# A gated convolution on one core: fifteen six-step groups instead of thirteen, one written list for all engines, and a wait between GpSimd's sums

## The chip, the cores and the metric

The kernel runs on one core of one Trainium2 chip. The metric is the device time of one execution in microseconds. Three runs of the kernel before gave 263.25, 263.71 and 264.98 us, a median of 263.71.

## The reference: what is computed

A WaveNet layer: a causal convolution over time with three taps at a dilation of 2, a gate, and a product with an output matrix. `x` is 2 x 16000 x 256, `w` is 3 x 256 x 512, `w_o` is 256 x 256, all bf16.

```
xp = jnp.pad(x, ((0, 0), (4, 0), (0, 0)))
h = xp[:, 4:4 + T] @ w[0]
for i in range(1, 3):
    off = 4 - i * 2
    h = h + xp[:, off:off + T] @ w[i]
f, g = h[..., :256], h[..., 256:]
return (jnp.tanh(f) * sigmoid(g)) @ w_o
```

## The kernel before

The time steps are cut into groups, and the convolution is not computed tap by tap but from sums and differences of input rows, which saves products. A group of kind B takes 4 rows of time at each of up to 256 places (R), 1024 time steps, and needs four products: `first` from the operand `m`, `last` from `p`, `zero` from `d0`, `inf` from `d3`. A group of kind A takes 6 rows at 256 places, 1536 steps, and needs five: `first` from `u1`, `mid` from `rm`, `last` from `rp`, `zero` from `r0`, `inf` from `ri`. The first group, of kind P, is computed tap by tap (`direct`). Before there are 13 A, 12 B (10 of them full, one of 160 and one of 128 places) and P.

Each group has four blocks, one for each 128 of the 512 output columns of `w`. A block is the unit of the schedule. On TensorE it has the products F (first), M (mid, A only), L (last), Z (zero) and I (inf), two matmuls each (`product`, line 401). The first four add up in one PSUM bank `b`, and between them the other engines take readings of it. After F, ScalarE copies `b` to `ss` (token c, line 432). After M, VectorE makes `hh` = 1.5 ss - b (h). After L, VectorE makes `a` = 3 ss + b in another bank (token a of the VectorE column), and `yy` = 2 hh + b (y). I adds into `a`. The rows of the output are then the bank `b` after Z, `yy` and `a`, through tanh or sigmoid on ScalarE (b, y, a; line 475). VectorE multiplies the two halves to `zz` (the gate, g, line 494). P is the output product, `zz` with `w_o`, four matmuls into `o_ps` (line 512). ScalarE casts it to `osb` (e, line 537), or VectorE does (v, line 521), and the SP queue stores it.

The operands come from a transposed input tile `xt`, which the SP queue loads. `m`, `p`, `d0`, `d3`, `u0`, `u1`, `u2`, `e`, `f` are sums or differences of two views of `xt`. `u3`, `uh`, `ud` are multiples of `u1`. `rp` is f + u1, `rm` is e + u3, `r0` is u0 + uh and `ri` is u2 + ud, each written on top of its first term (so in the profile rp's tile is named f, rm's e, and r0's and ri's u). Sums run on VectorE whole, or on GpSimd in quarters of 128 x 256 (`pre`, line 382). `rm`, `rp` and `r0` are made by an accumulating DMA that GpSimd issues (line 377), 13 of each; `ri` is made by GpSimd's sums.

The order is written by hand in PLAN. Each of its lines is the slot of one block and has four columns, for TensorE, ScalarE, VectorE and GpSimd. A block goes through several slots: F in its own, L in the next, Z and I in the one behind. `hold` makes a GpSimd sum wait for a given VectorE instruction: the last one before it in the program, or with one or two marks ' an earlier one. The blocks of the 25 groups of kinds A and B are taken in turn: four B groups first, then A and B mixed about two to one, the last B group at the end.

Of the kernel before, what the change touches and what calls it, by code (L numbers as in the profile page):

```python
# [11 lines left out]

PLAN = """
 |  | m.0 d3.0 p.0 d0.0 G | 
F D D | c w |  | 
F L D | c d | a d3.1 G | wa.4 wa.3
F L Z I P P | c b e | a | wa.6
Z L F I | a b c | m.1 d0.1 p.1 a | wa.12'
F L Z I | a c b | m.2 g a | wa.5
L P F Z I | a e c b | d3.2 a | wa.2'  # L20
Z L F I | a b c | d0.2 u0.0 g a | wa.7
F L Z I | a c b | f.0 u1.0 a | wa.1
L F Z I | a c b | p.2 a u2.0 g | wa.14'
L Z F I P | a b e c | e.0 d3.3 a | wa.0
F P P Z L I | a c e e b | p.3 ud.0 g a | wa.11
L F I Z P P | a c b | u1.1 m.3 m.4 a | rp.0 ri.0'
F L Z P I P | a e e e b c | u3.0 e.1 uh.0 a d0.3 f.2 g | wa.10
F I Z L P | a c e b | u1.2 a | rm.0 ri.0'
L F Z I | a e c b | a g | r0.0
L Z I F P | a b c | u3.1 p.4 a | wa.8  # L30
Z L F P I | a b c e e | u0.1 uh.2 f.1 a d0.4 g | ri.0'
F I L P Z M P | c e a b | d3.4 u2.1 ud.1 a h | rp.1 rm.1 wa.15' wa.13' wa.9'
F Z L M I | a c e e b | g uh.1 a y h | d3.5' d3.5' ri.0'
P P Z F L I | y a b c | u3.2 e.2 a y | r0.1 ri.1 m.5
F L I Z M | a c y b | a u0.2 h | d0.5 d0.5
Z F L I M | a b c e | g a y h | r0.2 d0.5 ri.1
F P Z I L | a e c b y | g u2.2 a y | rm.2 ri.1 m.5' d0.5
F L P I Z M | a e c y b | a e.3 h | p.5
Z F I L M | a c b | g a y h | p.5 p.5 ri.1
P P F Z L I | a e e y c b | u0.3 a y | m.5 m.5'  # L40
L F I Z M | a c y b | ud.2 a u1.3 h | ri.2 ri.2'
Z P P F L I P M | a b e c e e | g u3.3 a y h | rp.2 p.5' p.6' d0.6'
F Z I L P | a e b c y | f.3 g a y | ri.2 d3.5
F L I Z M | a c y b | a u2.3 h | d3.5
Z F I L M P P | a c b e | g a y h | rp.3 rm.3 d0.6 ri.2
F Z I L P | a e e y b c | uh.3 e.4 ud.3 a y | d3.6 p.6 ri.3''
F L I Z M | a c y b | a u1.4 h | ri.3
Z F I L M P P P | a c b e | g a y h | m.6 d3.6
F Z P L I | a e y c b e e e | g u0.4 u3.4 f.4 a y | r0.3 ri.3 m.6''
F L P I Z M | a c y b | a ud.4 h | d0.6 d3.6 m.6  # L50
Z I F L | a b c | g a y | ri.3 m.6
F L P I Z M P | c a y b | u2.4 a h | ri.4' d3.6
F Z L I P M | a e e c b | e.5 uh.4 y a h | rp.4 p.6
F Z P L I | a y c b e e | g f.5 a y | rm.4 p.6' d0.6'
F P L Z M I | a c y b | g a h | r0.4 p.7 p.7 ri.4 d3.7 d3.7 m.7
F Z L P M I | a c e b e | u1.5 a y h | ri.4
I Z P L F P P | a e e b c y | u0.5 a y | ri.4
F L Z I M | a c b y | ud.5 u1.6 u2.5 a h u3.5 g | rp.5 ri.5''
F P Z L I P M | a c e e b | a y h | rm.5 d0.7 p.7
F Z I L P | a e y b c e | g uh.5 a y | m.7' ri.5  # L60
F L I Z P M | a c y b | g ud.6 a h | r0.5 ri.5' m.7'
F P Z L M I | a c b e e | e.6 uh.6 y a h | d3.7 d0.7
F P Z L I P | y e a b c | f.6 a y | m.7' ri.5
F L Z M I P | a c y b e | u0.6 g h u3.6 a | rp.6 p.7' d0.7' d0.7
F L P M Z I | a c e e e b | y a h | rm.6
Z I L F P | a y b c | u2.6 u1.7 a y g | m.8' m.8'
F P P L Z M I | a c e y b e e | g u3.7 a h | r0.6 ri.6' d3.7'
F Z L P I M | a c b | e.7 ud.7 a y h | p.8' ri.6' ri.6
F Z I L P P | a y b c | u0.7 u2.7 a y | p.8' ri.6'
F L P M Z I | a e c y e e b | uh.7 f.7 a h g | d0.8' ri.7'  # L70
Z I F L | a b c | u1.8 a y | rm.7 rp.7 m.8'
F P P L Z M I | a c e y b e | g a e.8 h | d3.8 ri.7
F Z I L M P | a c b e | g a y ud.8 h | p.8 d3.8 ri.7
F P Z I L P | a e c y b e | u3.8 f.8 a y | r0.7 d3.8' d0.8
L F I Z M P | a e c b y | a u0.8 h | d0.8 m.8
F Z P L P M I P | a c e e e b | e.9 g a y h | p.8 ri.7
Z F L I | a b c y | u1.9 g a y | rp.8 d3.8
F L I Z M P P | a c e b y | u2.8 ud.9 a h | rm.8 d0.8 d3.9'
Z F L P M P I P | a e c e e b | uh.8 g a y h | ri.8 ri.8
Z L F I | y a b e c | u3.9 u2.9 a y | r0.8 ri.8  # L80
F I Z L M P P | a c y b | f.9 u0.9 a h | ri.9' ri.8'
F L Z I M | a e e c b | g y a h | ri.9
F Z I L | y a b c e | f.10 g a y | rp.9 d0.9
F P P L Z M I | c a b y | u0.10 a h | rm.9 d0.9'
F Z I L P P M | a e c e b | e.10 g uh.9 y a h | r0.9 d3.9
F P Z L P I | a e e y b c e | m.9 u1.10 a y | ri.9' ri.9
F L I Z M P | c a e b y | p.9 a h | d0.9' d3.9' d3.9'
Z P F L I M | a b c e e | ud.10 g a y h | d0.9
F I Z P L P | a y b c | u2.10 g a y | rp.10 ri.10 d3.10 d0.10
F L I Z M | a c e y b | a u1.11 h |   # L90
Z P F L P I | a b c e | u3.10 g y uh.10 a | rm.10 ri.10'
F L P Z I M | a e c b e y | e.11 a u2.11 h | ri.10'
F I Z L P P M | c a e b | ud.11 f.11 a y u3.11 h | r0.10 ri.10'
F I Z L | a e c y b e | g uh.11 a y | d3.10 d0.10'
L P F P Z M I | a c b y | g a h | rm.11 d0.10 d3.10
F Z L I M P | a c e b | u1.12 a y h | ri.11' ri.11'
F Z I L | a e c b y | p.10 m.10 y a | rp.11 ri.11
L P F P Z M I | a c e b y e | a u3.12 u0.11 h f.12 g | d3.10
Z F P L I P M P | a c b e | a y h | r0.11 ri.11 d0.10
I F Z L P | a e y e b e c | g e.12 ud.12 y a | rm.12  # L100
F P P M Z L P I | c e a b y e | p.11 u2.12 uh.12 a h g | d3.11' ri.12'
F I L P Z M P | a c e b | y a h | d0.11 d3.11
F Z L P I | y e a b c e e | u0.12 m.11 a y | rp.12 r0.12 ri.12''
F P Z L M I | c a b y | a h g | 
F Z L P I M P | a c b e e e | a y h | d0.11 ri.12
F Z L P I | a c b e y | g a y | d3.11 ri.12
L F I Z M P | a c y b e e | a g h | 
Z F L P I P M | b c a | y a h | 
F P Z L I | a e e y b c e | y a | d0.11
F P L Z M I | c a b y | a h g | d0.11  # L110
F P L Z I P | a e c b e | a y | d3.11
F I Z L | a c y b | g a | 
L P I F Z P | a e b c e | a g | 
Z I F L P P | a c b E | a v | 
L Z I P p | a b | a g v | 
Z I P p P | a e b | v | 
H H | a e E | g v | 
R R |  |  | 
 | e | v | 
# [4 lines left out]
def kernel(  # L124
# [7 lines left out]

    nc = tc.nc
# [15 lines left out]
    LOAD = 15  # L151
# [4 lines left out]
    LEAD, TRAIL = 4, 0  # L156
    N_A = (6, 7)
    groups, of_kind = [], {"P": [], "A": [], "B": []}

    def group(kind, b, t, R):  # L160
        of_kind[kind].append(len(groups))
        groups.append(dict(kind=kind, b=b, t0=t, R=R, J=ROWS[kind]))
        return t + ROWS[kind] * R

    for b in range(B):
        t = 0
        if b == 0:
            t = group("P", b, 0, 160)
        rows = (T - t - 6 * RG * N_A[b]) // 4
        n_a, n_b = N_A[b], rows // RG - (0 < rows % RG < P)  # L170
        for n in range(max(n_a, n_b)):
            if n < n_b:
                t = group("B", b, t, RG)
            if n < n_a:
                t = group("A", b, t, RG)
        rows = (T - t) // 4
        while rows:
            t = group("B", b, t, 160 if rows % P else P)
            rows = (T - t) // 4
    As, Bs = of_kind["A"], of_kind["B"]  # L180
    mixed = [[(g, oi) for g in gs for oi in range(4)] for gs in (As, Bs[LEAD:-1 - TRAIL])]
    seq = [(g, oi) for g in Bs[:LEAD] for oi in range(4)]
    took = [0, 0]
    while took != [len(m) for m in mixed]:
        nxt = 0 if took[0] * len(mixed[1]) < took[1] * len(mixed[0]) else 1
        seq.append(mixed[nxt][took[nxt]])
        took[nxt] += 1
    seq += [(g, oi) for g in Bs[-1 - TRAIL:] for oi in range(4)]
    slot_of = {blk: n for n, blk in enumerate(seq)}
    N = len(seq)  # L190
    assert N == 4 * (len(groups) - 1) == len(slot_of)
    begin = {g: slot_of[g, 0] for g in As + Bs}
    end = {g: slot_of[g, 3] for g in As + Bs}
# [323 lines left out]
    def out_evict(g, rb0, jp, on_v=False):  # L517
# [205 lines left out]
```

## Time and profile before

| what | value |
|---|---|
| median of three runs | 263.71 us |
| span of the profiled execution | 261.4 us |
| what lies around the span, median less span | 2.3 us |
| TensorE busy | 256.5 us, 98% |
| ScalarE busy | 243.7 us, 93% |
| VectorE busy | 240.5 us, 92% |
| GpSimd busy | 136.2 us, 52% |

The profile was taken of one execution; its own time outside the span is not shown, so the difference of the median and the span stands for it. An engine's busy time counts the time in which at least one of its instructions is shown at work. Instructions of one engine overlap by some 0.1 us, so the sum of the durations is larger than the busy time, and the distance between the starts of two neighbours is what one takes of its engine.

### The profile page before, as it was taken

The page shows a single profiled execution, that of the slowest core. Times are in us where ns is not written, and L with a number is a line of the kernel's source. Part 1 is how long each engine was busy: PE and PEld are TensorE (multiplying, and loading weights), DVE is VectorE, ACT ScalarE, POOL GpSimd, SP SyncE. Part 2 cuts the span into 40 slices and gives each one's busy share as a digit, 9 for nine tenths or more (in the row PEclk, how much of TensorE's full clock was granted, in tenths as well). Part 3 has the DMA queues.
Part 4 walks back from the last instruction along what each step waited for, and adds up shares of the span by engine and source line. Part 5 has one row for each costly group of instructions (what it writes and reads, how often), then busy time and mean ns, then how long its engine had stood idle before and what let it go on. Part 6 is the DMA issues. An engine that isn't in the chain of part 4 may idle for free.

```text
span 261.4 us, 4534 instructions
## 1 busy us (share of the span) xinstructions
PE 256.5 (98%) x1484; PEld 144.2 (55%) x1484; DVE 240.5 (92%) x401; ACT 243.7 (93%) x492; POOL 136.2 (52%) x204
## 2 busy tenths in 40 slices
PE   8999999999999999999999999999999999999993
PEld 5654565545545555555555555555555555665682
DVE  2899999999999999999999999999999999977773
ACT  4989998999999999999999999999999999999993
POOL 1033355687765577956757685643746453431100
PEclk9999999999999999999999999999999999999999
DMA  6999979999969667969895799959825574462115
GB/s 185 215 168 212 262 177 174 227 211 179 212 152 232 139 147 143 228 147 230 197 197 135 175 214 190 239 160 201 237 41 127 149 152 116 129 160 109 76 61 210
DMA packets 81663, 45.20 MB, mean 173 GB/s; under 512 B 68936, under 2 KB 70216, under 8 KB 81640
## 3 DMA queue, kind: packets, MB, share of 16 engines
q1 hardware_dynamic: 75112, 33.74, 54.6%
q0 software_dynamic: 5616, 10.23, 23.2%
q10 hardware_dynamic: 912, 0.95, 1.1%
q8 instruction: 11, 0.18, 0.3%
q14 instruction: 12, 0.10, 0.1%
HBM read 1.25 MB, written 16.38 MB: 67 GB/s over the span
## 4 chain that ended last, share of the span: by engine, by line
PE 97%; DMA 1%; DVE 0%; issue 0%
PE b L401 57%; PE o_ps L512 21%; PE a L401 16%; PE b L421 1%; PE a L421 1%; DMA xn<-in_x_dram 1%; PE tp L308 0%; DVE osb L521 0%; PE fill L248 0%
## 5 line engine op out<-in xcount | busy, mean ns | idle before, releaser
L435 DVE SCALAR_TENSOR_TENSOR a<-ss,b 128x512 f32<-128x512 f32 (+2 forms) x100 | 67.1, 672 | 7.9 <-ACT sg L475 3.1
L537 ACT CAST osb<-o_ps 128x512 bf16<-128x512 f32 x119 | 69.8, 622 | 0.8 <-PE o_ps L512 0.7
L512 PE MATMUL o_ps<-wo_sb,zz 128*128 128x256 bf16 x496 | 70.5, 273 | 0.0
L432 ACT COPY ss<-b 128x512 f32<-128x512 f32 (+2 forms) x100 | 59.6, 597 | 4.6 <-PE b L401 3.5
L512 PEld LDWEIGHTS <-zz 128*128 128x128 bf16 x496 | 48.4, 98 | 25.2 <-DVE zz L494 0.2
L401 PEld LDWEIGHTS <-w_sb 128*128 128x128 bf16 x400 | 39.0, 98 | 36.8 <-issue 0.2
L382 POOL TENSOR_TENSOR u<-u,ud 128x256 bf16<-128x256 bf16 x52 | 39.8, 772 | 24.9 <-DVE zz L494 9.1
L382 POOL TENSOR_TENSOR d<-xt 128x256 bf16<-128x256 bf16 (+2 forms) x56 | 33.4, 606 | 32.7 <-DVE zz L494 13.0
L494 DVE TENSOR_TENSOR zz<-th,sg 128x1536 bf16<-128x1536 bf16 (+2 forms) x52 | 40.9, 788 | 0.5 <-ACT sg L475 0.2
L435 DVE SCALAR_TENSOR_TENSOR yy<-hh,b 128x512 f32<-128x512 f32 x52 | 35.4, 680 | 1.9 <-PE b L401 1.8
L435 DVE SCALAR_TENSOR_TENSOR hh<-ss,b 128x512 f32<-128x512 f32 x52 | 35.4, 681 | 1.2 <-PE o_ps L512 0.5
L475 ACT ACTIVATE sg<-b 128x512 bf16<-128x512 f32 (+2 forms) x50 | 30.5, 610 | 2.1 <-PE b L401 1.4
L475 ACT ACTIVATE th<-b 128x512 bf16<-128x512 f32 (+2 forms) x50 | 30.5, 610 | 1.9 <-PE b L401 1.6
L475 ACT ACTIVATE sg<-a 128x512 bf16<-128x512 f32 (+2 forms) x50 | 31.0, 619 | 0.0
L401 PE MATMUL b<-f,wp_sb 128*128 128x512 bf16 x104 | 30.9, 379 | 0.0
L401 PE MATMUL b<-u,w_sb 128*128 128x512 bf16 x104 | 30.9, 379 | 0.0
L401 PE MATMUL a<-u,w_sb 128*128 128x512 bf16 x104 | 30.9, 379 | 0.0
L401 PE MATMUL b<-u,wa_sb 128*128 128x512 bf16 x104 | 30.9, 379 | 0.0
L401 PE MATMUL b<-e,wm_sb 128*128 128x512 bf16 x104 | 30.9, 378 | 0.0
L475 ACT ACTIVATE th<-a 128x512 bf16<-128x512 f32 (+2 forms) x50 | 30.5, 614 | 0.3 <-PE a L401 0.2
L401 PEld LDWEIGHTS <-wp_sb 128*128 128x128 bf16 x200 | 19.5, 98 | 20.1 <-issue 0.7
L401 PEld LDWEIGHTS <-wm_sb 128*128 128x128 bf16 x200 | 19.5, 98 | 17.0 <-issue 0.4
(59 smaller groups left out, 342.7 us busy)
## 6 DMA issues: line engine op xcount, KB each, us to landing
out_dram<-osb SPq DMA_DIRECT2D x26, 384.0 KB, 2.6
out_dram<-osb SPq DMA_DIRECT2D x23, 256.0 KB, 3.0
f<-u POOLq DMA_DIRECT2D x13, 256.0 KB, 3.5
e<-u POOLq DMA_DIRECT2D x13, 256.0 KB, 4.4
u<-uh POOLq DMA_DIRECT2D x13, 256.0 KB, 5.3
w_sb<-in_w_dram ACTq DMA_DIRECT2D x3, 256.0 KB, 4.1
xt<-in_x_dram SPq DMA_TRANSPOSE x25, 7.2
xn<-in_x_dram SPq DMA_DIRECT2D x1, 160.0 KB, 3.2
```

What stands on the lines that cost most here:

```text
L382: ins = eng.tensor_tensor(out=o, in0=a, in1=b, op=op)
L401: nc.tensor.matmul(G[bank, oi][:, :2 * R], lhsT=wmat[:, ct, osl], rhs=G[mv][:, :, ct, :R], start=which == "first" and ct == 0, stop=ct == ...
L421: nc.tensor.matmul(G[bank, oi][:, :4 * r].rearrange("p (j r) -> p j r", j=4), lhsT=w_taps[tap][:, ct, osl], rhs=xt[:, j0:j0 + 4, ct, c0 + ...
L432: nc.scalar.copy(out=G["ss", oi][:, :n], in_=G["b", oi][:, :n])
L435: return note(nc.vector.scalar_tensor_tensor(out=out, in0=in0, scalar=scalar, in1=in1, op0=ALU.mult, op1=op))
L475: nc.scalar.activation(out=G[name, dt][:, j:j + 2, :R], in_=G[bank, oi][:, :2 * R].rearrange("p (q r) -> p q r", q=2), func=(ACT.Tanh, ACT ...
L494: note(nc.vector.tensor_tensor(out=G["z"][:, dt, :, :n], in0=G["th", dt][:, :, :n], in1=G["sg", dt][:, :, :n], op=ALU.mult))
L512: nc.tensor.matmul(o_ps[:, q, :], lhsT=z, rhs=wo_sb[:, dt, :], start=dt == 0 and (q == 0 or len(dts) == NT), stop=dt == NT - 1, skip_group ...
L537: copy(out=osb[:, 2 * jp:2 * jp + 2, :], in_=o_ps[:])
```

## The change

**Groups.** The table GROUPS sets them: in the first batch P, seven A, four full B and one B of 128 places; in the second eight A, three full B and one B of 160. That makes 15 A, 9 B (7 of them full) and P, 96 blocks instead of 100. ORDER gives the turn of the blocks: three B groups first, then A and B mixed three to one, the B of 128 at the end.

**One list.** PLAN is now one list of tokens for all engines, 1744 of them, in the order in which the program issues them. A token with a point names an operand: `u1.5q1` is one quarter of u1 of the sixth A group on GpSimd, which waits for the VectorE instruction that stands one back from the last; `rp.13d` is an accumulating DMA; `u3.4` is made by VectorE. In the list are also the loads (x) and the stores (s). Two lines of it:

```diff
+h51 e.14q53 P b I A u2.13q19 e96 L y f.13q26 F s37 Y Z a u0.14q15 I b A P rp.13d c F a rp.14d L c Z ri.13d A I r0.13
+b Z y M u3.14 v97 F b e.14q1 a P h52 I u2.14q14 y F c g e.14q54 L e98 P Y c M e99 d3.8q30 A P e.14q96 y M h53 s38 P
```

**Who does what.** `hh` is made by VectorE as before in 34 of the 60 blocks of kind A. In the other 26 (k) ScalarE copies `b` to `hh`, and VectorE makes `yy` = a - 2 hh, which reads the bank `a` before I adds to it. VectorE casts 28 outputs instead of 5. More of the sums of `xt` run on GpSimd, and `ri` is an accumulating DMA in 14 groups: there are 55 such DMAs instead of 39.

**The wait on GpSimd.** `settle` makes the second sum behind a DMA's issue wait for the end of the first.

**Buffers.** The pools of the operands are replaced by rings with the same number of places (`slot`), and the first weights' parts `wu` take the places of the first `zz` tiles instead of those of `hh` and `yy`.

```diff
+GROUPS = (
+    "P160 A A A A A A A B B B B B128",
+    "A A A A A A A A B B B B160",
+)
...
+    on_pool = []
+
+    def settle(ins, piece):
+
+        if piece and len(on_pool) > 1 and on_pool[-1][1] and not on_pool[-2][1]:
+            tc.add_manual_dep(
+                ins.ins, on_pool[-1][0].ins.name,
+                mybir.DependencyInfo(mybir.DependencyClass.Sync, mybir.DependencyReason.DATA),
+                reason="GpSimd's cores come together behind a DMA's issue",
+            )
+        on_pool.append((ins, piece))
+        return ins
...
-        if name in BY_DMA:
-            return nc.gpsimd.dma_start(out=G[name][:, :, :, :R], in_=b, accum_op=op)
+                G[name] = slot(name, G["n"], [P, 2, CT, RG])
+        if eng is None:
+            return settle(nc.gpsimd.dma_start(out=G[name][:, :, :, :R], in_=b, accum_op=op), False)
...
+        if eng is nc.gpsimd:
+            settle(ins, True)
         return hold(ins, behind)
...
-    def halfway(blk):
+    def second(blk, on_act):
...
-        G["hh", oi] = ss_pool.tile([P, 2 * RG], f32, name="hh")
+        G["hh", oi] = slot("hh", a_seq.index(blk), [P, 2 * RG], f32)
+        if on_act:
+            G["k", oi] = True
+            nc.scalar.copy(out=G["hh", oi][:, :n], in_=G["b", oi][:, :n])
+            return
...
-            stt(G["y", oi][:, :n], G["hh", oi][:, :n], 2.0, b)
+            if ("k", oi) in G:
+                stt(G["y", oi][:, :n], G["hh", oi][:, :n], -2.0, G["a", oi][:, :n])
+            else:
+                stt(G["y", oi][:, :n], G["hh", oi][:, :n], 2.0, b)
...
+    def on_gpsimd(token):
+        token, _, back = token.partition("q")
+        behind = made_v[-1 - int(back)]
...
+        had = quarters.get((g, name), 0)
+        quarters[g, name] = had + 1
+        pre(g, name, nc.gpsimd, slice(had, had + 1), behind=behind)
```

The order on VectorE in the middle of the mixed blocks, before (numbers behind the names tell tiles apart):

```order
L435 SCALAR_TENSOR_TENSOR hh_1433<-ss_1403,b_1400 128x512
L382 TENSOR_TENSOR e_1459<-xt_1049 128x1024
L380 TENSOR_SCALAR uh_1461<-u1_1254 128x1024
L435 SCALAR_TENSOR_TENSOR yy_1463<-hh_1433,b_1400 128x512
L435 SCALAR_TENSOR_TENSOR a_1467<-ss_1403,b_1400 128x512
L435 SCALAR_TENSOR_TENSOR hh_1469<-ss_1442,b_1439 128x512
L494 TENSOR_TENSOR zz_1331<-th_1380,sg_1446 128x1024
L382 TENSOR_TENSOR f_1496<-xt_1049 128x1024
L435 SCALAR_TENSOR_TENSOR a_1501<-ss_1442,b_1439 128x512
```

and a like place now:

```order
L328 TENSOR_SCALAR ud_1235<-u1_942 128x1024
L328 TENSOR_SCALAR uh_1237<-u1_1113 128x1024
L330 TENSOR_TENSOR u2_1243<-xt_820 128x1024
L452 TENSOR_TENSOR zz_1093<-th6_1142,sg6_1178 128x1536
L385 SCALAR_TENSOR_TENSOR a_1265<-ss_1208,b_1193 128x512
L385 SCALAR_TENSOR_TENSOR yy_1276<-hh_1227,a_1265 128x512
L479 CAST osb4_1281<-o_ps_1260 128x512
L385 SCALAR_TENSOR_TENSOR a_1291<-ss_1247,b_1232 128x512
L328 TENSOR_SCALAR ud_1304<-u1_1113 128x1024
L385 SCALAR_TENSOR_TENSOR yy_1309<-hh_1267,a_1291 128x512
```

The sums from SBUF stand together now, and behind them those that read PSUM. The blocks shown have no hh on VectorE, `yy` reads `a` and comes behind it, and a cast stands between.

The order on GpSimd, before, with the semaphores for which each waits:

```order
L382 TENSOR_TENSOR u2_914<-u2_914,ud_1039 128x256 [waits DVE_49]
L382 TENSOR_TENSOR d3_786<-xt_634 128x256
L382 TENSOR_TENSOR d3_786<-xt_634 128x256 [waits DVE_49]
L377 DMA f_1124<-u1_1045 128x1024 [waits DMASW1_49]
L377 DMA e_952<-u3_1089 128x1024 [waits DMASW2_49]
L382 TENSOR_TENSOR d0_1095<-xt_982 128x256 [waits DVE_49]
```

and now:

```order
L325 DMA e_807<-u3_899 128x1024 [waits DMASW4_49,Pool_49]
L325 DMA f_736<-u1_710 128x1024 [waits DMASW5_49,Pool_49]
L325 DMA f_1076<-u1_942 128x1024 [waits DVE_49]
L325 DMA u2_1063<-ud_912 128x1024 [waits DMASW7_49]
L330 TENSOR_TENSOR u1_1113<-xt_820 128x256 [waits DMASW1_49,DMAHW5_49,DVE_49,PE_49]
L330 TENSOR_TENSOR u1_1113<-xt_820 128x256 [waits Pool_49]
L330 TENSOR_TENSOR d3_854<-xt_662 128x256
L330 TENSOR_TENSOR d0_962<-xt_662 128x256
```

Four DMAs are issued in a row, the second sum behind them waits for GpSimd's own semaphore, and the quarters of different operands alternate. Sums that wait for VectorE (DVE) have become fewer: 36 of 172 rows, where it was 89 of 149.

More of the change, by code (lines that the diff above doesn't have):

```diff
@@ L120 @@
+v118 a P e119 Z P e120 P b s46 e121 P g s45 v122 H e123 H R R s47 v124 e125 s48
 """
@@ L209, with slot @@
     ctx.enter_context(tc.manual_schedule())
+    SLOTS = {"m": 2, "p": 2, "d0": 3, "d3": 3, "u0": 3, "u1": 3, "u2": 3, "e": 3, "f": 3, "u3": 2, "uh": 2, "ud": 2, "hh": 3, "th": 2, "osb": 3, "odd": 3}
+    def slot(name, n, shape, dtype=bf16, kind=None):
+        return ring_pool.tile(shape, dtype, name=name, tag=f"{name}.{n % SLOTS[kind or name]}")
     def warm_up(n):
@@ L276 @@
     wm_sb = consts.tile([P, CT, D2], bf16)
-    wu_sb = [[ss_pool.tile([P, D2], f32, name=f"wu{tap}", tag=tag) for tag in ("hh", "yy")] for tap in range(K)]
+    wu_ct = [z_pool.tile([P, K, D2], f32, name="wu", tag="zz6") for _ in range(CT)]
+    wu_sb = [[wu_ct[ct][:, tap, :] for ct in range(CT)] for tap in range(K)]
     wa_sb = consts.tile([P, CT, D2], bf16)
@@ L351, in operand @@
         }[name]()
+    blocks = [0] + [g for g, oi in seq if oi == 3]
+    a_seq = [blk for blk in seq if blk[0] in As]
+    on_pool = []
[8 more added lines that the diff above has]
+        return ins
     def hold(ins, behind):
@@ L362 @@
     ON_TOP = {"rp": "f", "rm": "e", "r0": "u0", "ri": "u2"}
-    BY_DMA = ("rm", "rp", "r0")
     def pre(g, name, eng, qs=slice(0, 4), behind=None):
@@ L465, in activate @@
         if (name, dt) not in G:
-            G[name, dt] = act_pool.tile([P, J, RG], bf16, name=name, tag=f"{name}{J}")
+            same = [at for at in blocks if groups[at]["J"] == J]
+            G[name, dt] = slot(f"{name}{J}", NT * same.index(g) + dt, [P, J, RG], kind="th")
         if G["kind"] == "P":
@@ L705 @@
+    assert next(todo, None) is None and next(to_load, None) is None
 _INS = ['x', 'w', 'w_o']
```

403 lines of the change are left out of this document (141 added, 262 removed).

## The prediction

> **What bounds the kernel now.** I read the page first, for the shares of the engines and the chain that ended last.
>
> ```profile
> span 261.4 us, 4534 instructions
> PE 256.5 (98%) x1484; PEld 144.2 (55%) x1484; DVE 240.5 (92%) x401; ACT 243.7 (93%) x492; POOL 136.2 (52%) x204
> PE 97%; DMA 1%; DVE 0%; issue 0%
> ```
>
> TensorE is busy 98% of the span, and the chain of waits is TensorE for 97% of it. A share over the whole span hides stages, so the busy time in stretches of 20 us comes next. Its columns are the stretch, its length, the busy time and instructions of PE, PEld, DVE, ACT and POOL, the granted clock, the DMA share and GB/s.
>
> ```profile
> 20.00:40.00 20.00, 20.00 (x111) 10.64 (x109) 19.83 (x34) 18.69 (x38) 8.60 (x12) 1.00 1.01 221
> 100.00:120.00 20.00, 20.00 (x114) 10.95 (x113) 19.61 (x32) 19.49 (x40) 15.34 (x22) 1.00 0.84 188
> 180.00:200.00 20.00, 20.00 (x116) 11.14 (x115) 19.52 (x33) 19.30 (x40) 10.57 (x15) 1.00 0.63 152
> 220.00:240.00 20.00, 20.00 (x125) 12.01 (x123) 17.51 (x31) 19.88 (x44) 7.18 (x12) 1.00 0.46 125
> 250.00:261.40 11.40, 7.30 (x67) 6.20 (x64) 6.17 (x12) 7.22 (x19) 0.00 (x0) 0.98 0.41 155
> ```
>
> TensorE never stops between 20 and 240 us, at the full clock. VectorE and ScalarE are nearly as full: 19.5 to 19.8 and 18.7 to 19.9 of 20 us. So three engines are close to the limit, TensorE first, and only GpSimd has room. A little less work on TensorE pays only as long as the other two keep up.
>
> The busy columns count overlapping instructions, so what one instruction really takes of its engine is read from the distance of starts in the timeline:
>
> ```profile
> 99.99 0.69 DVE L435 SCALAR_TENSOR_TENSOR hh<-ss,b 128x512 f32<-128x512 f32 x1
> 100.59 0.68 DVE L494 TENSOR_TENSOR zz<-th,sg 128x1024 bf16<-128x1024 bf16 x1
> 101.19 0.69 DVE L382 TENSOR_TENSOR f<-xt 128x1024 bf16<-128x1024 bf16 x1
> 101.37 1.08 ACT L537 CAST osb<-o_ps 128x512 bf16<-128x512 f32 x2
> 101.45 0.59 PE L401 MATMUL a<-u,w_sb 128*128 128x512 bf16 x2
> 101.88 0.59 PE L401 MATMUL b<-u,wa_sb 128*128 128x512 bf16 x2
> 102.31 0.60 PE L512 MATMUL o_ps<-wo_sb,zz 128*128 128x256 bf16 x4
> 102.31 0.64 ACT L475 ACTIVATE sg<-a 128x512 bf16<-128x512 f32 x1
> 102.80 0.63 ACT L432 COPY ss<-b 128x512 f32<-128x512 f32 x1
> 103.00 0.95 DVE L494 TENSOR_TENSOR zz<-th,sg 128x1536 bf16<-128x1536 bf16 x1
> 103.27 0.69 ACT L475 ACTIVATE th<-yy 128x512 bf16<-128x512 f32 x1
> 103.81 0.64 ACT L475 ACTIVATE th<-b 128x512 bf16<-128x512 f32 x1
> 103.87 0.69 DVE L435 SCALAR_TENSOR_TENSOR a<-ss,b 128x512 f32<-128x512 f32 x1
> ```
>
> Two matmuls of 512 columns take 101.88 - 101.45 = 0.43 us, 0.215 each. A VectorE instruction takes 0.60 (0.87 for the wide gate zz), a ScalarE cast or copy 0.47, an activation 0.49 (0.54 from yy).
>
> **TensorE: the term that carries the sum.** Its products by kind of group, in the groups of lines kept apart by shape:
>
> ```profile
> L401 PE MATMUL a<-u,w_sb 128*128 128x512 bf16 x104 | 30.9, 379 | 0.0
> L401 PE MATMUL a<-d,w_sb 128*128 128x512 bf16 x80 | 23.8, 379 | 0.0
> ```
>
> A six-step group (A) has five products of 8 matmuls, 40 for 1536 rows; 104/8 makes 13 of them. A four-step group (B) has four products, 32 matmuls for 1024 rows; 80/8 makes 10 full ones, with one of 160 and one of 128 columns, which stay. Now there are 15 A and 7 full B: 2x40 more, 3x32 fewer, so 16 matmuls of 512 columns go. The output products stay at 500. 16 x 0.215 = **3.4 us** less, in a stage where TensorE never stops.
>
> **VectorE and ScalarE: both a little less.** By the order, VectorE loses 4 sums into a, 18 of hh, 14 full operand sums (87 to 73) and 6 gates of 1024, and gains 8 sums into yy and 23 casts of outputs: -42 + 31 = -11 at 0.60 is -6.6 us. Six scalings more (their row is below) at 0.34, which is their mean of 0.42 less the 0.08 by which the others overlap, are +2.0, four wide gates at 0.87 are +3.5, small ones about -0.8. Sum: **-1.9 us**. ScalarE loses 23 casts and 4 copies (27 x 0.47 = 12.7) and 8 activations (3.9), and gains 26 copies into hh (12.2) and 8 activations from yy (4.3): **about -0.3 us**, with one small cast.
>
> ```profile
> L380 DVE TENSOR_SCALAR u<-u 128x1024 bf16<-128x1024 bf16 x13 | 5.5, 423 | 0.0
> ```
>
> Neither is on the chain; what they need is shown to be tight by the windows, and that is a rival below.
>
> In 26 of 60 blocks ScalarE's copy replaces VectorE's hh, and yy then reads a. So the "inf" product into a must wait for two VectorE sums (1.2 us) instead of one. In the list it stands at least 0.43 us behind yy's place and mostly 1.3. Bounds: 0 if other products fill this, 26 x 0.17 (0.60 less 0.43) = 4.4 us if all stood at the shortest. Six do, which is 1.0 us; half of it lies within the list's step of 0.43. I take 0.3.
>
> **GpSimd and its DMAs.** Sums on quarters go from 124 wide and 16 small to 140 and 24, accumulating DMAs from 39 to 55 (ri now goes by DMA too). Rows of such a place:
>
> ```profile
> 113.88 0.87 POOL L377 DMA_DIRECT2D e<-u  x1 [1.06 <-DVE u L380]
> 114.54 0.86 POOL L382 TENSOR_TENSOR d<-xt 128x256 bf16<-128x256 bf16 x1
> 115.11 0.91 POOL L382 TENSOR_TENSOR p<-xt 128x256 bf16<-128x256 bf16 x1
> L382 POOL TENSOR_TENSOR u<-u,ud 128x256 bf16<-128x256 bf16 x52 | 39.8, 772 | 24.9 <-DVE zz L494 9.1 <-DVE yy L435 4.4 <-DVE u L382 3.5
> ```
>
> A DMA's issue takes 0.66 us of GpSimd. 24 sums at up to 0.77 and 16 issues at 0.66 add at most 29 us to 136.2: 165 of 261, still with room. The new wait (27 sums name GpSimd's own semaphore) has no row; the sums behind an issue took 0.86 and 0.91 us and started 0.57 apart. At worst the second one starts at the first one's end, 0.3 us later, 27 x 0.3 = 8 us; at best the two no longer stretch each other and it gains 0.2 each. Both lie in GpSimd's room. Behind the waiting sum stand the other quarters and the next DMA's issue, for which a product waits.
>
> That product is the real exposure. From a DMA's place in the list to the first product that reads its tile I counted the product tokens between, at 0.43 us. The shortest are rp.13 with 3.8 us and r0.14 with 3.9, then rm.0, rm.11 and rm.12 with 4.3, rp.2 with 4.8, rm.3 and rm.6 with 5.2; the other 47 have 5.6 and more. The time from issue to landing, from the page:
>
> ```profile
> f<-u POOLq DMA_DIRECT2D x13, 256.0 KB, 3.5
> e<-u POOLq DMA_DIRECT2D x13, 256.0 KB, 4.4
> u<-uh POOLq DMA_DIRECT2D x13, 256.0 KB, 5.3
> DMA to landing us min/median/max: 3.3/4.4/10.9
> ```
>
> At the minimum of 3.3 nothing is late. At the medians rp (f, 3.5) is in time, three rm (e) are 0.1 late each and r0.14 is 1.4 late. r0.14 is the last accumulate, when no input load is left, so it is nearest to the minimum. Bounds 0 and 6.6 us (all eight at 5.3: 1.5 + 1.4 + 3 x 1.0 + 0.5 + 2 x 0.1); I take **0.2**.
>
> The Trainium skill, "DMA: Bandwidth & Descriptors", section "Anatomy of one DMA — SWDGE (gpsimd) path", gives a fit of 2.0 us and the bytes over 436 GB/s. By it 256 KB would land in 2.6 us (an estimate), no DMA would be late, and this term would be 0; the trace's shortest 3.3 is above that, so the trace decides.
>
> **The sum.** The profiled execution's span is 261.4; the runs shown have a median of 263.71, so 2.3 us lie around the span. 261.4 - 3.4 + 0.3 + 0.2 = 258.5, and with 2.3 around it **260.8 us**. The start (direct products of the first group) and the end (last gate, casts, store) are the same steps in both.
>
> **Rivals.** *ScalarE sets the pace.* It had 19.3 to 19.9 of 20 us busy from 100 us on, and keeps its work (-0.3 us) in 1.3% less time. Counting both lists in stretches of eight blocks at the distances above, ScalarE has 0.95 of TensorE's work (0.99 at worst, blocks 32 to 40) against 0.93 before (1.02 at worst). For: the thin margin. Against: the worst stretch is better than before's, which TensorE passed without stopping. If the pace is ScalarE's, only its 0.3 is saved: 263.4 us.
>
> *Accumulating DMAs land late.* This is the slower side. It decides where landing takes over 4.3 us for the five shortest leads; at 5.3 the cost is the 6.6 us above on top of 260.3: 266.9 us, less if the first stalls give the later ones more lead. For: the medians of e and u<-uh, and 55 DMAs for 39 on one queue. Against: no input load stands beside most of the short leads in the list.
>
> *GpSimd meets VectorE.* Before, 89 of 149 rows of GpSimd's sums wait for VectorE, now 36 of 172. Where sums meet, both grow:
>
> ```profile
> L382 POOL TENSOR_TENSOR u<-u,ud x52: 658/667/1125, 33.1 to 236.4; 128x256 bf16<-128x256 bf16 x52
> L382 DVE TENSOR_TENSOR u<-xt x39: 673/685/1215, 21.7 to 227.8; 128x1024 bf16<-128x1024 bf16 x39
> ```
>
> 0.46 us on GpSimd, 0.53 on VectorE. VectorE has about 5% of 220 us, some 11 us, in hand; 20 meetings use it up, and 30 would cost 30 x 0.53 - 11 = 5 us: 265.3 us. Against: in the list 131 of 184 sums come right behind a VectorE instruction that reads PSUM, one for one.
>
> The Trainium skill, "SBUF — State Buffer", section "Who interferes with whom", says that a VectorE instruction with two SBUF inputs and a GpSimd one that reads SBUF exclude each other, and the second blocks fully. The two maxima above agree. By this rule fewer waits would mean more blocking; it is the ground of this rival, and its price stands in the rows.
>
> That the products do not fall in number is excluded by the order: the matmuls are counted there.
>
> **How the numbers follow.** The forecast has 0.62, and with its own terms it spans 259.2 to 262.3 (no added waits and a little less at the end, to both waits at twice my values and one more microsecond). About 1% can be told from no change here: 2.6 us, so 261.07. Of the forecast 0.52 lies below that, 0.10 above. ScalarE's pace has 0.18, late DMAs 0.12, meetings 0.08. Faster by over 1%: 0.52; within: 0.10 + 0.18 = 0.28; slower by over 1%: 0.20. The range takes in the first three cases up to about the late DMAs' time: 259.0 to 266.0.
>
> **What would show it.** Right: 824 wide matmuls of the two kinds, PE still at 20.00 of 20 in the stretches, its busy sum near 253, the span near 258.5. ScalarE's pace: TensorE gaps of 0.1 to 0.5 us all along, released by ScalarE. Late DMAs: a few gaps of 1 us and more in front of products from f, e or u. Meetings: VectorE's sums at 0.9 us and more in mean. Wrong altogether: a span above 262.

## The result and the profile after

The changed kernel took 262.28 us in the median of 13 runs (261.86 to 262.71), the kernel before 263.35 in 13 runs beside it (262.81 to 264.98). The ratio is 0.9958 with a 95% interval of 0.9946 to 0.9971: 0.42% or 1.07 us faster. Here and below, a ratio leaves out executions that took over 1.5% longer than the fastest one of the same kernel. The forecast was 260.8 us. The direction is right and the time lies in the range, but well under half of the gain came, and the gain is within the 1% to which the prediction gave 0.28.

The page of the changed kernel, the span, the busy times and the chain of waits:

```profile
span 260.3 us, 4591 instructions
...
PE 253.9 (98%) x1468; PEld 142.0 (55%) x1468; DVE 242.7 (93%) x398; ACT 242.9 (93%) x490; POOL 170.8 (66%) x248
...
PE 79%; DVE 13%; issue 2%; DMA 2%; ACT 2%; ACTq 1%; POOL 1%; DVEq 0%
```

TensorE is busy 2.6 us less, but the chain of waits is now TensorE for 79% of it and VectorE for 13%; before it was TensorE for 97%. VectorE was to have 1.9 us less work and is busy 2.2 us longer. The profiled execution took 262.04 us, so 1.7 us lie around its span.

The busy times in stretches, with the columns as before and one stretch more (140 to 160 us):

```profile
20.00:40.00 20.00, 19.78 (x107) 10.21 (x106) 19.80 (x36) 18.38 (x38) 11.33 (x17) 1.00 1.13 223
100.00:120.00 20.00, 20.00 (x116) 11.07 (x115) 19.93 (x32) 19.74 (x41) 16.86 (x22) 1.00 0.94 188
140.00:160.00 20.00, 19.46 (x107) 10.27 (x106) 19.66 (x33) 18.55 (x37) 15.72 (x21) 1.00 0.93 199
180.00:200.00 20.00, 20.00 (x110) 10.58 (x109) 19.55 (x33) 19.33 (x39) 17.54 (x27) 1.00 0.67 159
220.00:240.00 20.00, 20.00 (x121) 11.74 (x120) 19.10 (x31) 19.43 (x41) 14.80 (x23) 1.00 0.45 106
250.00:260.30 10.30, 5.97 (x55) 5.09 (x53) 4.72 (x10) 6.02 (x14) 0.00 (x0) 0.97 0.48 180
```

TensorE is not at 20 of 20 everywhere any more, and VectorE is fuller than before between 100 and 120 us (19.93 for 19.61). The products themselves have fallen as forecast:

```profile
L351 PE MATMUL a<-u,w_sb 128*128 128x512 bf16 x120 | 35.5, 379 | 0.0
...
L351 PE MATMUL a<-d,w_sb 128*128 128x512 bf16 x56 | 16.5, 379 | 0.0
```

120/8 makes 15 groups A and 56/8 makes 7 full groups B, 824 wide matmuls. The busy column hides small waits, since the profile models the ends of matmuls. I read the waits from the starts: where the next matmul starts later than the one before it by more than its pitch (0.215 us for 512 columns, 0.109 for 256), TensorE has waited for the difference. Summed in this way TensorE's own work fell from 252.4 to 249.0 us, by 3.45, and its waits rose from 1.4 to 3.8 us. By what ended them, the waits for VectorE rose from 0.5 to 3.1 us, those for a DMA from 0 to 0.4, and those for ScalarE fell from 1.0 to 0.4. So 3.45 less 2.4 gives the gain of 1.1.

Why VectorE is late shows in its groups of lines kept apart by shape. Of the kernel before:

```profile
L382 DVE TENSOR_TENSOR u<-xt 128x1024 bf16<-128x1024 bf16 x39 | 27.9, 720 | 0.0
L494 DVE TENSOR_TENSOR zz<-th,sg 128x1536 bf16<-128x1536 bf16 x26 | 24.8, 954 | 0.5 <-ACT sg L475 0.2
...
L380 DVE TENSOR_SCALAR uh<-u 128x1024 bf16<-128x1024 bf16 x13 | 5.5, 420 | 0.0
```

and of the changed one:

```profile
L452 DVE TENSOR_TENSOR zz<-th,sg 128x1536 bf16<-128x1536 bf16 x30 | 32.1, 1073 | 0.0
...
L330 DVE TENSOR_TENSOR u<-xt 128x1024 bf16<-128x1024 bf16 x28 | 19.3, 701 | 0.0
...
L328 DVE TENSOR_SCALAR uh<-u 128x1024 bf16<-128x1024 bf16 x15 | 7.5, 500 | 0.0
```

The same instruction on the same shape takes longer in mean: the wide gate 1073 ns for 954, the scaling 500 for 420. The plain sums u did not, at 701 for 720. The timeline of the changed kernel at its largest group of waits shows single instructions that are lengthened:

```profile
147.58 0.66 POOL L330 TENSOR_TENSOR e<-xt 128x256 bf16<-128x256 bf16 x1 [0.99 <-PE b L351]
147.66 0.87 DVE L328 TENSOR_SCALAR uh<-u 128x1024 bf16<-128x1024 bf16 x1
...
148.19 0.59 PE L351 MATMUL b<-d,w_sb 128*128 128x512 bf16 x2
148.32 1.27 POOL L330 TENSOR_TENSOR u<-xt 128x256 bf16<-128x256 bf16 x2
...
148.44 0.67 DVE L385 SCALAR_TENSOR_TENSOR hh<-ss,b 128x512 f32<-128x512 f32 x1
...
149.04 1.36 DVE L452 TENSOR_TENSOR zz<-th,sg 128x1536 bf16<-128x1536 bf16 x1
149.17 0.59 PE L351 MATMUL b<-f,wp_sb 128*128 128x512 bf16 x2 [0.38 <-DVE hh L385]
...
150.90 0.59 PE L351 MATMUL b<-u,wa_sb 128*128 128x512 bf16 x2
...
151.65 0.59 PE L351 MATMUL b<-u,w_sb 128*128 128x512 bf16 x2 [0.15 <-DVE yy L385]
```

GpSimd's sum of e starts at 147.58 and runs for 0.66; VectorE's uh starts 0.08 behind it and takes 0.87 instead of 0.42. So hh starts late, and the next product waits: 149.17 - 148.19 - 0.43 = 0.55 us. The gate zz meets the sums of u and takes 1.36 instead of 0.95; the products behind it lose 0.32 (151.65 - 150.90 - 0.43) and 0.17 more. Over the whole kernel I add up what each VectorE instruction takes above the usual duration of its shape (the 15th percentile of the same kernel). This **stretch** is 4.3 us before and 10.1 after. Of the rise of 5.8 us, 5.5 lie on instructions that read SBUF alone (from 2.89 to 8.35); 31 of them are lengthened by over 0.06 us after, 10 before. Those that read PSUM went from 1.4 to 1.8.

Which of the two engines starts first decides which of them pays. In the changed kernel 28 VectorE instructions that read SBUF alone start while a sum of GpSimd still has over 0.1 us to run, and together they lose 7.4 of the 8.35 us; before there were 17, which lost 2.2. The gate at 149.04 starts with 0.54 us of such a sum left and takes 0.41 longer, uh at 147.66 with 0.58 left and takes 0.46 longer. Where VectorE starts first, it loses under 0.2 us in all, and GpSimd's sum is the one that grows: 42 sums of GpSimd started under such an instruction after, 41 of them lengthened, and 39 before, all lengthened (three that start in its last 0.01 us are not counted). So the meetings in which GpSimd comes second hardly rose in number; those in which VectorE comes second did.

### The profile page after: what moved, and what is told of

Its sections match the earlier page's. It is cut to its first block, busy times and chain, and to the rows that moved or that the text cites. A ratio compares the mean times of both kernels' runs of the same rounds, so it can differ in the third digit from the quotient of the medians.

```text
span 260.3 us, 4591 instructions
## 1 busy us (share of the span) xinstructions
PE 253.9 (98%) x1468; PEld 142.0 (55%) x1468; DVE 242.7 (93%) x398; ACT 242.9 (93%) x490; POOL 170.8 (66%) x248
## 4 chain that ended last, share of the span: by engine, by line
PE 79%; DVE 13%; issue 2%; DMA 2%; ACT 2%; ACTq 1%; POOL 1%; DVEq 0%
PE b L351 46%; PE o_ps L470 18%; PE a L351 12%; DVE a L385 4%; DVE zz L452 2%; DVE yy L385 2%; DMA e<-u 2%; DVE u L330 1%; PE b L371 1%; PE a L371 1%; DVE hh L385 1%; DVE uh L328 1%; ACTq L189 1%; POOL wu L233 1%; DVE d L330 1%
## 5 line engine op out<-in xcount | busy, mean ns | idle before, releaser
L385 DVE SCALAR_TENSOR_TENSOR a<-ss,b 128x512 f32<-128x512 f32 (+1 forms) x96 | 64.0, 668 | 5.8 <-PE b L351 4.5
L382 ACT COPY ss<-b 128x512 f32<-128x512 f32 (+1 forms) x96 | 56.1, 591 | 5.2 <-PE b L351 4.4
L487 ACT CAST osb<-o_ps 128x512 bf16<-128x512 f32 x96 | 57.6, 617 | 0.9 <-PE o_ps L470 0.4
L330 POOL TENSOR_TENSOR u<-xt 128x256 bf16<-128x256 bf16 x68 | 50.5, 757 | 6.1 <-PE b L351 4.7
L351 PE MATMUL b<-f,wp_sb 128*128 128x512 bf16 x120 | 35.7, 379 | 0.4 <-DVE hh L385 0.4
L351 PE MATMUL b<-e,wm_sb 128*128 128x512 bf16 x120 | 35.7, 379 | 0.2 <-DMA e<-u 0.2
L351 PE MATMUL b<-u,w_sb 128*128 128x512 bf16 x120 | 35.7, 379 | 0.2 <-DVE yy L385 0.2
L330 POOL TENSOR_TENSOR e<-xt 128x256 bf16<-128x256 bf16 x24 | 19.7, 823 | 12.2 <-PE b L351 6.7
L330 POOL TENSOR_TENSOR f<-xt 128x256 bf16<-128x256 bf16 x28 | 21.5, 773 | 6.4 <-DVE ud L328 2.8
L385 DVE SCALAR_TENSOR_TENSOR hh<-ss,b 128x512 f32<-128x512 f32 x34 | 23.0, 678 | 0.5 <-PE b L351 0.2
```

Of the source, the lines that this page charges most:

```text
L330: ins = eng.tensor_tensor(out=o, in0=a, in1=b, op=op)
L351: nc.tensor.matmul(G[bank, oi][:, :2 * R], lhsT=wmat[:, ct, osl], rhs=G[mv][:, :, ct, :R], start=which == "first" and ct == 0, stop=ct == ...
L382: nc.scalar.copy(out=G["ss", oi][:, :n], in_=G["b", oi][:, :n])
L385: return note(nc.vector.scalar_tensor_tensor(out=out, in0=in0, scalar=scalar, in1=in1, op0=ALU.mult, op1=op))
L487: copy(out=G["osb", at][:, 2 * jp:2 * jp + 2, :], in_=o_ps[:])
```

## The experiments

The theory was: GpSimd's sums meet VectorE's instructions that read SBUF, these grow, and TensorE waits for VectorE. Its rivals were: the work on VectorE is simply too much, ScalarE sets the pace, the new wait on GpSimd costs the time, or the DMAs are late. The ratios are against the kernel before, with 95% intervals.

**GpSimd writes, but reads nothing.** Each of GpSimd's sums is replaced by two fills with a constant, with the same waits around them. The operands made there are then constants.

```diff
+        elif eng is nc.gpsimd:
+            hold(settle(eng.memset(o, 0.01), True), behind)
+            ins = eng.memset(o, 0.01)
+            on_pool[-1] = (ins, True)
+            return ins
...
-        if eng is nc.gpsimd:
-            settle(ins, True)
```

> The changed kernel, with each of GpSimd's sums on operands replaced by two fills of the same quarter with a constant: GpSimd is busy for about as long and writes the same tiles, but reads nothing from SBUF (the operands are then constants, and GpSimd no longer waits for the input's loads). Theory 1, GpSimd's reading sums and VectorE's instructions with SBUF inputs hold each other up, VectorE comes late (10.1 us of stretch where it was 4.3) and TensorE waits 3.1 us for it: the stretch falls under 4 us, TensorE waits under 1.5 us in all, and the time is 1.2 to 2.5 us under the changed kernel's 262.3, so 259.8 to 261.1. Theory 2, the list has too little room on VectorE by itself: TensorE still waits 3 us or more and the time stays within 0.5 us of 262.3. Theory 3, the wait between GpSimd's sums: no change either, since the wait stays.

It took 260.58 us, ratio 0.9895 (0.9879 to 0.9912).

```profile
span 258.5 us, 4740 instructions
...
PE 253.0 (98%) x1468; PEld 142.4 (55%) x1468; DVE 237.5 (92%) x398; ACT 242.3 (94%) x490; POOL 152.9 (59%) x416
```

```profile
L455 DVE TENSOR_TENSOR zz<-th,sg 128x1536 bf16<-128x1536 bf16 x30 | 28.4, 949 | 0.0
...
L328 DVE TENSOR_SCALAR uh<-u 128x1024 bf16<-128x1024 bf16 x15 | 6.6, 439 | 0.0
```

The page and the two groups of VectorE: the gate's duration is back where it was and the scaling's nearly (439 ns for 420), VectorE is busy 5.2 us less, its stretch is 3.3, and TensorE waits for it 1.0 us instead of 3.1. In all TensorE waits some 1.6 us, a little over the expected 1.5. The span is the forecast's 258.5. So nearly all of the 1.7 us by which this run is faster lie in the reading by GpSimd beside VectorE; the wait for a DMA at 35.9 us also shrank, from 0.38 to 0.12. GpSimd also had less to do (152.9 us for 170.8), and its fills are shorter than its sums. What separates the two is what a meeting does: here eleven gates start while a fill has over 0.1 us to run, and none is lengthened by more than 0.011 us.

The same edit on the kernel before is the control.

> The kernel before, with the same replacement of GpSimd's sums by fills. Theory 1: TensorE waited only 0.5 us for VectorE there, so at most 0.5 us to win, 262.8 to 263.4. Theories 2 and 3: no change, 263.3.

It took 264.33 us, ratio 1.0036 (1.0005 to 1.0066). Its executions scattered, and the profiled one took 964.69 us, so its trace shows nothing of the meetings. The same kernel was measured once more.

> The kernel before, with GpSimd's sums replaced by fills that read nothing, once more, since its first runs scattered from 262.9 to 269.8. If meetings cost the kernel before little (TensorE waited 0.5 us for VectorE in it), 262.7 to 263.4; the same edit took 1.7 us off the changed kernel.

264.01 us, ratio 1.0027 (1.0008 to 1.0045), some 0.6 us above the expected range. The stretch fell from 4.3 to 2.4 us and TensorE's waits for VectorE from 0.5 to 0.3, so at most 0.2 us were there to win. But the control is not a clean one: in its profiled execution one accumulating DMA landed late, and by the starts TensorE waited 0.74 us for it, at 111.5 us. The wait at its idle part:

```profile
PE b L405 <- DMA u<-uh: 0.6, 1, 0.6
```

The fills by themselves make the kernel before no faster. Why that DMA was late there is not shown.

**Without the wait on GpSimd.**

```diff
-        if piece and len(on_pool) > 1 and on_pool[-1][1] and not on_pool[-2][1]:
+        if False and len(on_pool) > 1 and on_pool[-1][1] and not on_pool[-2][1]:
```

> The changed kernel without the wait between the first and the second sum behind a DMA's issue; all else the same. Theory 1 and theory 2: the wait is off the path or helps a little to keep the quarters in step with VectorE: -0.2 to +0.6 us against the changed kernel's 262.3. Theory 3, the wait is what eats the gain: 0.8 to 2.4 us faster.

275.33 us, ratio 1.0448 (1.0416 to 1.048): 13 us slower than with it, which none of the theories expected. The page, and what TensorE waited for:

```profile
span 274.8 us, 4593 instructions
...
PE 259.5 (94%) x1468; PEld 143.3 (52%) x1468; DVE 254.5 (93%) x398; ACT 244.5 (89%) x490; POOL 165.4 (60%) x248
```

```profile
PE o_ps L470 <- DVE zz L452: 4.5, 3, 3.2
PE a L351 <- DVE yy L385: 2.5, 4, 1.3
PE b L351 <- DVE hh L385: 2.4, 3, 1.1
```

The worst place of it in the timeline:

```profile
169.56 1.17 POOL L325 DMA_DIRECT2D u<-uh  x1
...
170.17 3.66 POOL L330 TENSOR_TENSOR u<-xt 128x256 bf16<-128x256 bf16 x5
...
171.57 4.69 DVE L452 TENSOR_TENSOR zz<-th,sg 128x1024 bf16<-128x1024 bf16 x1
...
172.82 0.27 PE L470 MATMUL o_ps<-wo_sb,zz 128*128 128x256 bf16 x1
...
173.22 1.22 POOL L330 TENSOR_TENSOR e<-xt 128x256 bf16<-128x256 bf16 x1
...
173.85 1.79 POOL L330 TENSOR_TENSOR u<-xt 128x256 bf16<-128x256 bf16 x2
...
175.06 2.34 POOL L330 TENSOR_TENSOR e<-xt 128x256 bf16<-128x256 bf16 x2
...
176.32 1.68 PE L470 MATMUL o_ps<-wo_sb,zz 128*128 128x256 bf16 x7 [3.23 <-DVE zz L452]
```

A gate of 1024, 0.71 us in mean in the changed kernel, takes 4.69 here, from 171.57 to 176.26. In this time GpSimd starts seven more sums of the run behind the DMA's issue, the last at 175.68, and TensorE stands for 3.2 us. In such a run the sums start some 0.6 us apart (170.17, 170.81, 171.43) and take 1.2 us, so that each overlaps the next. Counting only sums of 128 x 256 that overlap no VectorE instruction reading SBUF, those at the second to sixth place behind an issue take 0.76 to 0.82 us in mean without the wait, and 0.64 to 0.66 with it. The stretch of GpSimd's sums is 41.9 us here, and 28.2 in the changed kernel. The wait on GpSimd is therefore not a cost: without it the change makes the kernel slower than before.

The Trainium skill, "SBUF — State Buffer", section "Who interferes with whom", says that a VectorE instruction with two SBUF inputs and a GpSimd one that reads SBUF exclude each other, but not one that only writes, and that the second blocks until the first is through. The fills above agree with the first half (gate 949 ns), and so does the split by who starts first. The 4.69 us go further than the second: the gate waits out not one GpSimd instruction but a whole run of overlapping ones.

**The wait added to the kernel before.** The same `settle`, which doubles the rows of sums that name GpSimd's own semaphore, from 15 to 31.

```diff
+            return settle(nc.gpsimd.dma_start(out=G[name][:, :, :, :R], in_=b, accum_op=op), False)
...
+        if eng is nc.gpsimd:
+            settle(ins, True)
...
-                hold(weights_a(2 * K + int(token[3:])), behind)
+                hold(settle(weights_a(2 * K + int(token[3:])), True), behind)
```

> The kernel before, with the changed kernel's wait alone: the second sum behind a DMA's issue waits for the first to end. Without this wait the changed kernel took 275.3 us: its sums behind an issue stayed long in whole runs (0.82 to 1.00 us each up to the seventh) and VectorE was held up for as long as a run lasted. Theory A, that needs runs of GpSimd sums without another wait, and the kernel before breaks its runs by the waits for VectorE: no change, 262.9 to 263.7, and the stretch on VectorE stays near 4 us. Theory B, every pair behind an issue costs: the stretch falls by 1 us or more and the time by 0.5 us or more.

263.13 us, ratio 1.000 (0.9987 to 1.0014), with a stretch of 5.2 us for 4.3. There the wait gives nothing. Most sums of that kernel wait for VectorE anyway (89 of 149 rows), and long runs are rare: behind 3 of 35 issues four or more sums follow one another without a gap of 0.1 us, against 17 of 32 in the changed kernel. So the wait is worth 13 us in the one kernel and nothing in the other.

**The wait between every two sums.**

```diff
-        if piece and len(on_pool) > 1 and on_pool[-1][1] and not on_pool[-2][1]:
+        if piece and len(on_pool) > 1 and on_pool[-1][1]:
```

> The changed kernel, with the wait between every two neighbouring sums on GpSimd, not only behind a DMA's issue. Theory A, one wait brings the sums into step and they stay so: nothing to win, each wait costs GpSimd some time, so the sums slide against VectorE's and the time is 0 to 3 us above 262.3. Theory B, each pair of overlapping sums holds VectorE up longer than one sum would: the stretch on VectorE falls from 10 to under 7 us and the time by 0.5 to 1 us.

268.16 us, ratio 1.0169 (1.0144 to 1.0193), 5.9 us above the changed kernel, more than either theory allowed. GpSimd falls behind, and now DMAs land late (waits of TensorE):

```profile
PE a L351 <- DMA u<-ud: 1.4, 1, 1.4
PE b L351 <- DVE a L385: 1.2, 3, 0.8
```

By the starts TensorE waits 2.7 us for DMAs and 6.0 for VectorE.

**Sums held behind VectorE.** First every sum of GpSimd waits for the VectorE instruction just ahead in the list, so that it starts beside one that reads PSUM where the list has it so; then only those whose neighbour ahead reads SBUF, 45 by the rule of the edit.

```diff
-        pre(g, name, nc.gpsimd, slice(had, had + 1), behind=behind)
+        pre(g, name, nc.gpsimd, slice(had, had + 1), behind=made_v[-1])
```

> The changed kernel, with every sum on GpSimd waiting for the VectorE instruction that stands just ahead of it in the list, as the kernel before did for most. Theory 1: GpSimd's sums start again with a VectorE instruction that reads PSUM, the stretch on VectorE falls to 4 to 7 us and TensorE's waits for VectorE to 1 to 2 us; if GpSimd's DMAs do not come late by it, 0.5 to 1.5 us faster than 262.3, else the gain goes into waits for DMAs. Theory 2: no gain on VectorE, and GpSimd later, so 0 to 2 us slower.

266.95 us, ratio 1.0143 (1.0129 to 1.0158), slower than either theory expected.

```diff
+    reads_sbuf = [False]
...
-        pre(g, name, nc.gpsimd, slice(had, had + 1), behind=behind)
+        pre(g, name, nc.gpsimd, slice(had, had + 1), behind=made_v[-1] if reads_sbuf[0] else behind)
...
+        if "." in token and "q" not in token and token[-1] != "d" or what in "gG":
+            reads_sbuf[0] = True
+        elif what in "AYhv" and "." not in token:
+            reads_sbuf[0] = False
```

> The changed kernel, where a GpSimd sum that stands in the list right behind a VectorE instruction with SBUF inputs waits for that instruction; the others keep the list's own waits. If meetings are what eats the gain and come from GpSimd starting one VectorE instruction too early, the stretch on VectorE falls to 5 to 8 us and the time to 261.3 to 262.0. If the later GpSimd then meets VectorE further on, as when all sums waited (266.95 us, 17 us of stretch), the time is 262.5 to 265.

264.14 us, ratio 1.0034 (1.0023 to 1.0045). Both are slower than the changed kernel; neither is a cure. The stretch did not fall, it rose (table below). A held sum comes later and runs on into the next instruction: the VectorE instructions reading SBUF that start with over 0.1 us of a sum of GpSimd left rise from 28 to 51 with all sums held and to 43 with some, while the sums of GpSimd that start under such an instruction fall from 42 to 28 and 15. The hold moves the cost from GpSimd to VectorE.

**Seven hh more copied by ScalarE,** to relieve VectorE between blocks 28 and 40 (k in place of h).

```diff
-h32 Z a v63 e.9q32 L c I f.9q200 b A M u1.10q16 a Y P y u1.10q39 F h33 Z rp.9d c g L b rm.9d I Y y L ri.9d a A F P
+k32 Z a v63 e.9q32 L c I f.9q200 b A M u1.10q16 a Y P y u1.10q39 F h33 Z rp.9d c g L b rm.9d I Y y L ri.9d a A F P
```

> The changed kernel, with seven more of the hh in the blocks between 135 and 175 us (28, 29, 31, 32, 35, 39, 40 of the A blocks) copied by ScalarE instead of summed by VectorE: 4.2 us less on VectorE, 3.3 us more on ScalarE, where ScalarE was busy 18.6 and 19.3 of 20 us. If VectorE's lateness is what TensorE waits for there (1.1 us between 140 and 160), the waits there fall under 0.5 us and the time is 0.3 to 0.9 us under 262.3. If ScalarE is as full as it looks, TensorE waits for it instead and the time stays within 0.3 us or rises.

263.05 us, ratio 0.9988 (0.9977 to 0.9999), slower than the changed kernel. The stretch 140 to 160 us:

```profile
140.00:160.00 20.00, 19.54 (x107) 10.20 (x106) 17.78 (x28) 19.77 (x41) 15.84 (x22) 1.00 0.92 185
```

VectorE now has room (17.78 of 20) and the waits for it there are gone, but ScalarE is full (19.77 for 18.55), and TensorE's waits for ScalarE rise from 0.4 to 1.8 us in all. So there is no slack on ScalarE to take over work of VectorE in that stretch.

**Five sums moved.** At the four worst meetings five sums of GpSimd start behind the VectorE instruction that they met. Three of them wait for a later instruction, two are moved in the list as well. One of the edits:

```diff
-u1.10q5
+u1.10q0
```

> The changed kernel, with five of GpSimd's sums made to start behind the VectorE instruction with SBUF inputs that they met in its profile, at the four places where TensorE then waited (near 48, 70, 148 and 210 us: 0.2 + 0.3 + 1.0 + 0.3 us). Nothing else in the list is changed. If these meetings are what TensorE waits for, and GpSimd has room for the five delays, TensorE's waits for VectorE fall from 3.1 to 1.3 to 2.0 us and the time to 261.0 to 261.9. If the delayed sums only meet the next instruction, as when 37 were held (264.1 us), the time is 262.0 to 263.0.

261.89 us, ratio 0.9943 (0.9926 to 0.9961). The wait at 71 us is gone, those between 148 and 152 us fall from 1.04 to 0.33, that at 211 us from 0.33 to 0.08; new ones of 0.40 and 0.27 us appear at 80 and 214 us. In all TensorE waits 2.8 us for VectorE, where 1.3 to 2.0 were expected. The wait for a DMA at 35.9 us, ahead of all five edits, is missing in this execution, which is worth 0.4 us by itself. This is the fastest kernel with the whole computation that was run, but its interval overlaps that of the changed kernel: not told apart from it.

All kernels that share the list of the change, by the stretch of VectorE:

| kernel | stretch of VectorE, us | TensorE waits for VectorE, us | span, us |
|---|---|---|---|
| GpSimd writes only | 3.3 | 1.0 | 258.5 |
| five sums moved | 9.7 | 2.8 | 260.1 |
| changed kernel | 10.1 | 3.1 | 260.3 |
| held behind SBUF readers | 12.0 | 4.5 | 261.9 |
| wait between all sums | 12.8 | 6.0 | 266.4 |
| all sums held | 17.0 | 7.6 | 265.2 |
| no wait | 22.1 | 14.8 | 274.8 |

The kernel with more copies is left out, since it changes VectorE's work too. The waits follow the stretch in order: from the first row to the third 6.8 us of stretch cost 2.1 us of waiting, from the third to the last 12.0 cost 11.7. Where the order of the spans differs from that, the late DMAs of the wait between all sums are the cause (2.7 us).

## Why the prediction was right and wrong

**TensorE's term was right.** 824 wide matmuls and 3.45 us less work, for the 3.4 forecast.

**The failing step is the rival "GpSimd meets VectorE", and with it the pricing of VectorE as off the path.** The sum has no term for these meetings, and they cost 2.6 us: TensorE's waits for VectorE rose from 0.5 to 3.1. The prediction named the mechanism and its rows, but gave VectorE "some 11 us in hand", from its mean idle share, to be used up before the first microsecond counts. The stretch rose by 5.8 us, about half of that, and TensorE waited all the same. VectorE's idle time is not in hand where the meeting takes place: the windows shown between 100 and 200 us have it at 19.5 to 19.9 of 20 us (the two between them at 19.0), and a product waits for hh, yy or zz within a microsecond or two. A meeting costs where it happens. What spoke against the rival, that 131 of 184 sums come right behind a VectorE instruction that reads PSUM, is a fact of the list; GpSimd runs by its own waits, and a sum that starts beside a reader of PSUM can still be at work when the next VectorE instruction, a reader of SBUF, starts. The count of waits said nothing of that either: the sums that waited for VectorE started behind it and paid themselves, and it is VectorE's starts under a running sum that rose, from 17 to 28. The rival's own price, 265.3 us with 30 meetings, did not come either: 31 instructions were lengthened, but by 0.25 us each in mean and not 0.53, which is the price of the longest one. Nor did its sign, VectorE's sums at 0.9 us in mean: the sums u take 0.70, and it was mostly the gates and scalings that grew. Its chance stood in the wrong place too: 265.3 us is within 1% of 263.71, so its 0.08 belonged to "within", which makes that 0.36, and "slower" 0.12.

**VectorE's and ScalarE's work.** The forecast had VectorE at 1.9 us less and ScalarE at 0.3 less. ScalarE went from 243.7 to 242.9. VectorE rose from 240.5 to 242.7; without GpSimd's reading beside it, it is 237.5, 3.0 less, of which 1.0 is stretch that the kernel before had (4.3 for 3.3). So the count of instructions was fair, and the durations taken from the kernel before did not hold in the new neighbourhood.

**The wait on GpSimd** was costed between 8 us at worst and a gain of 0.2 each, all in GpSimd's room. Its worth is 13 us, shown by taking it away, and it lies mostly in VectorE: TensorE waits 14.8 us for it without, 3.1 with. The prediction looked at what the wait delays on its own engine, and not at what the sums that it separates would do to another.

**Late DMAs** cost 0.38 us for the forecast 0.2, at one place: rm.0, at 35.9 us, one of the three for which e's landing stood just above the lead. The wait is shown at its idle part:

```profile
PE b L351 <- DMA e<-u: 0.2, 1, 0.2
```

All other DMAs were in time. The median of f grew from 3.5 to 4.2 us, those of e and of u<-uh fell from 4.4 to 4.1 and from 5.3 to 4.7, and u<-ud (ri) is new:

```profile
f<-u POOLq DMA_DIRECT2D x14, 256.0 KB, 4.2
e<-u POOLq DMA_DIRECT2D x14, 256.0 KB, 4.1
u<-ud POOLq DMA_DIRECT2D x14, 256.0 KB, 5.6
u<-uh POOLq DMA_DIRECT2D x13, 256.0 KB, 4.7
```

The rival of 266.9 us did not come about; it did come in part with a wait between every two sums. (Its figure leaves out the 0.3 us of the inf product that the sum has; with it, it would be 267.2.)

**The inf product behind yy** waited some 0.5 us for it (0.19 at 49.6 and at 55.2 us, 0.10 at 99.3) for the forecast 0.3. Most of that belongs to the meetings: where GpSimd reads nothing, 0.14 us are left, so the term was if anything too large. **ScalarE's pace** did not set the time: its waits fell. It would have, had seven more copies been given to it.

**Around the span** lie 1.7 us and not 2.3: the median of three runs was 263.71, that of 13 is 263.35, and the span of 261.4 came from a run whose own time was not known (later executions of the kernel before have 1.7 to 1.8 us around theirs, as 263.25 for a span of 261.5). With 1.7 around its span of 258.5 the forecast would have been 260.2, further from the measured time; the writes-only kernel, which has that span, took 260.31 in its profiled execution. So this term did not cause the miss, it hid 0.6 us of it.

## What to carry to other kernels

The idle share of an engine is no reserve against a longer instruction: look at whether the instructions behind it are waited for at that place, and price a meeting there at its full length once the stretch of the timeline is full. When instructions move between VectorE and GpSimd, list the pairs that both read SBUF and will run side by side, and ask which of the two will start first, since the other one pays; durations from the old neighbourhood don't carry over. And a wait that looks like a cost on an idle engine may be what keeps it from holding up a busy one: try it both ways, and in both kernels, before calling it either.

## What the runs showed of the hardware that was not expected

A VectorE gate or sum that starts under a sum of GpSimd takes longer by what is left of that sum, less 0.12 to 0.13 us. This holds for all 21 that start in the changed kernel with over 0.1 us left: at 111.20 us 0.61 us were left and the gate took 0.48 longer, at 134.28 0.50 and the sum m 0.38. Under a fill the gates lose at most 0.011 us; a scaling that starts with 0.22 us of a fill left still loses 0.08 (146.81 us of the run with fills).

GpSimd's sums that run on behind a DMA's issue overlap one another for the whole run, at 0.76 to 0.82 us each where sums behind one wait take 0.64 to 0.66. A VectorE gate that meets such a run is held for nearly the rest of it: 4.69 us at the longest, with a mean of 0.71 for its shape in the changed kernel. One wait behind the issue is enough to prevent it; a wait between every two sums is worse (268.16 us). That the cause is the issue leaving GpSimd's parts out of step is argued from these durations and not shown.
